# Linear attention followed by attention experts on one core: batch 0's k loads from ScalarE's queue, the table load behind them, fewer zero matmuls in front

## The chip, the core and the metric

The kernel runs on one core of one Trainium2 chip. TensorE (PE) multiplies matrices, VectorE (DVE), ScalarE (ACT) and GpSimd (POOL) work elementwise, and SyncE (SP) mostly starts transfers (DMA). Any of SyncE, ScalarE and GpSimd can start a transfer. Each engine works through its own list of instructions in order and waits on semaphores for the others. The metric is the device time of one execution in microseconds (us); the figure given is the median of the runs.

## The reference

```python
kv  = einsum('bhsd,bhse->bhde', k, v)          # batch 8, heads 8, seq 576, head_dim 64
o   = einsum('bhsd,bhde->bhse', q, kv)
x   = o / sqrt(mean(o*o) + 1e-6) * g_norm      # per head; heads side by side: (8, 576, 512)
logits = x @ w_gate                            # 4 experts, the best 2 of each token
for e in range(4):                             # causal attention of each expert
    a   = softmax(mask(scale * (x @ wq[e]) @ (x @ wk[e]).T))
    out += weight_of(e) * (a @ (x @ wv[e]) @ wo[e])
```

All inputs and the output are float32.

## The kernel before

The eight batches are worked one after the other, with neighbouring batches overlapping. The body of the kernel is a list of some 1,100 small tasks, each a name and indices, such as ("kv", 0, 2). The list's order is written out by hand in `ORDER`, and `ENGINE` says for every task which engine runs it (V, A, G, S, and C for ScalarE's own queue). The loop at the end (L840 to L844) walks through it and emits each task. So each engine's instructions stand in the order of the list, and an engine never passes one of its own instructions over to a later one.

Transfers in the front are cut small. k and v of one batch come as four loads each, `lk(b, p, z)` and `lv(b, p, z)`: p picks the heads (0 to 3 or 4 to 7), z the first 4 or the last 5 of the 9 neighbouring rows that go to one partition (256 KB for z = 0, 320 KB for z = 1). q comes as two loads `lq(b, u)` of 576 KB. `load` at L328 issues those of k and v on SyncE (L332), `lq` those of q (L347). Partitions of z = 0 have a fifth column that no load fills; it is set to zero by a memset (L218, L219, L223, L224), and the loads with z = 1 write into the same column and so wait for that memset.

The order in which batch 0 begins, with each task's engine, is this:

- SyncE: lv(0,1,0), lv(0,1,1), lk(0,1,1), lk(0,1,0), lq(0,1): the "first half", heads 4 to 7
- TensorE: kv(0,2), kv(0,3) (`kv`, L408): the products of k and v of heads 4 to 7, which need all four loads of p = 1
- ScalarE: kvc(0,1) (L419, the copy to `kvs` by `copy`, L311)
- SyncE: lv(0,0,0)
- ScalarE: kvx(0,3,1) (L424, a copy of 32 partitions to `kvm`)
- VectorE: kvx(0,1,1)
- SyncE: lk(0,0,1), lv(0,0,1)
- VectorE: kvx(0,2,1)
- SyncE: lk(0,0,0)
- ScalarE: kvx(0,0,1)
- TensorE: o(0,1) (`o_mm`, L442), which needs all of `kvs`, `kvm` and the transposed q (VectorE, L437)
- ScalarE: the squares of o (L470)
- TensorE: kv(0,0), kv(0,1), which need the "second half" of k and v, heads 0 to 3; then the sums of the squares (L482), from which the norm is worked out in turns of ScalarE and VectorE
- SyncE: lq(0,0), and then the loads of batch 1: lk(1,1,1), lv(1,0,1), lv(1,0,0), lk(1,0,0), lk(1,1,0), lv(1,1,0), lk(1,0,1), lv(1,1,1), the k weights, q of batch 1

Before some tasks stand zero matmuls (`zero_matmuls`, L826): products of a tile of zeros, written to a bank that the task behind them overwrites. `ZEROS` (L26) says before which task and how many. [...] ScalarE's table of functions is loaded by the instruction at L217, ahead of everything else on ScalarE.

Eight semaphores serve the transfers of SyncE and ScalarE in turn, in the order of the list. A transfer whose semaphore still belongs to an earlier one waits until that one has landed.

Of the kernel before, what the change touches and what calls it, by code (L numbers as in the profile page):

```python
# [23 lines left out]


ZEROS = {  # L26
    ("kv", 0, 2): 20, ("o", 0, 1): 6, ("kv", 0, 0): 2, ("o", 0, 0): 2,
}

ORDER = (  # L30
# [96 lines left out]
def kernel(  # L127
# [13 lines left out]
    nc = tc.nc  # L141
# [22 lines left out]
    order_only = mybir.DependencyInfo(mybir.DependencyClass.Sync, mybir.DependencyReason.DATA)  # L164
    begun = [0]
    moved = []

    def place(key, n=1):
        if key not in slot_of:
            at = begun[0]  # L170
            slot_of[key] = tuple(int(d, 16) for d in SLOTS[at : at + n])
            begun[0] += n
        return slot_of[key]
# [40 lines left out]
    kt, vt = [  # L214
        [sb.tile([P, H, LO + 1, Dh], FP32, tag=f"{m}{j}", name=f"{m}_b{j}") for j in range(2)] for m in "kv"
    ]
    nc.scalar.preload_act_table_set("natural_log_exp_and_others")  # L217
    nc.gpsimd.memset(vt[0][:, :, LO], 0.0)  # L218
    nc.vector.memset(kt[0][:, :, LO], 0.0)  # L219
    ident_f = const.tile([P, P], FP32, name="ident_f")  # L220
# [56 lines left out]
    for j in range(2):  # L277
        t = const.tile([P, NCH * S + PAD], FP32R, name=f"xT{j}")
        nc.vector.tensor_copy(out=t[:, NCH * S :], in_=zeros[:, 0:PAD])
        xTs.append(t)  # L280
    for j in range(3):
        t = const.tile([P, 2, strips + PAD], BF16, name=f"PT{j}")
        nc.gpsimd.memset(t[:, :, strips:], 0.0)
        PTs.append(t)
        t = const.tile([P, NB * P], FP32R, name=f"kT{j}")
        nc.vector.tensor_copy(out=t[:, S:], in_=zeros[:, 0:PAD])
        kTs.append(t)
    for j in range(2):
        t = const.tile([P, NB, 8], FP32, name=f"lg8_{j}")
        nc.gpsimd.memset(t[:], -1.0e30)  # L290
        lg8s.append(t)
        t = const.tile([P, NB, E, Hd + 1], BF16, name=f"vext{j}")
# [30 lines left out]
    def queued(task, ins):  # L323
        if len(task) > 1 and task[0] in ("lk", "lv", "lq") and task[1] > 1:
            tc.add_manual_dep(ins.ins, moved[-FLIGHT].name, order_only, reason="queue")
        moved.append(ins.ins)

    def load(m, dst, src, b, p, z):  # L328
        n, t0 = LO + z, LO * z
        hs = slice(4 * p, 4 * p + 4)  # L330
        rows = src[b, hs].rearrange("h (r t) d -> r h (t d)", t=RUN)[:, :, t0 * Dh : (t0 + n) * Dh]
        queued((m, b), nc.sync.dma_start(dst[z::2, hs, 0:n, :].rearrange("r h t d -> r h (t d)"), rows))  # L332

    def lk(b, p, z):
        load("lk", k_t(b), k, b, p, z)

    def lv(b, p, z):
        load("lv", v_t(b), v, b, p, z)
# [469 lines left out]
    def store(b, qc, *h):  # L808
# [8 lines left out]
        lk=lk, lv=lv, lq=lq, lgv=lgv, lwg=lwg, wgs=wgs, lw=lw, ws=ws, lwo=lwo, wo=wo, kv=kv, kvc=kv_copy, kvx=kv_move, qc=q_turn,  # L817
        o=o_mm, oc=o_copy, sq=square, ms=sums, G=gates, ln=ln, rs=rs, na=newton_a, nb=newton_b, lo=newton_c, R=newton_d,
# [7 lines left out]
    def zero_matmuls(n, count):  # L826
        if n[0] in ("kv", "v", "y", "ot", "lt", "ms", "G"):
            at = (kv_bank(*n[1:]) if n[0] == "kv" else small("v", n[1], n[2] // 2) if n[0] == "v" else small(*n))[0]
        elif n[0] in ("qp", "kp"):
            at = small(n[0][0], *n[1:])[0]  # L830
        elif n[0] == "o":
            at = big("o", n[1], n[2], 0)[0]
        else:
            at = big(*n)[0]
        for _ in range(count):
            use(nc.tensor.matmul(  # L836
                bank(at)[:, 2 * P : 3 * P], lhsT=zeros[:, 0:P], rhs=zeros[:], start=True, stop=True, skip_group_check=True
            ), at)

    with tc.manual_schedule():  # L840
        for n in order:
            if n in ZEROS:
                zero_matmuls(n, ZEROS[n])
            emit[n[0]](*n[1:])  # L844
# [30 lines left out]
```

## Time and profile before

| | |
|---|---|
| median of 3 runs | 202.35 us (202.04 to 202.89) |
| the profiled execution: its own time | 203.93 us |
| the profiled execution: its span, first to last instruction | 202.2 us |
| mean granted TensorE clock | 0.984 |
| batch 0's k loads, issued by SyncE at | 2.31, 2.96, 4.92, 6.80 us |

Times in the profile count from the start of the span. In a row of a timeline the first number is the start and the second the length in us, then come the engine, the line of the kernel, the operation and what it writes from what; "x2" says that two instructions in a row are merged, and the bracket gives the idle time before it and what ended it. "SPq" is SyncE issuing transfers, "PEld" TensorE's loading of weights. In a row of stretches each engine has its busy time and, in brackets, the number of instructions; behind them stand the granted TensorE clock as a share of full speed, the share of time that the 16 DMA engines were busy, and GB/s. In a list of transfers the last number is the time from issue to landing. In a list of who waited for whom, the numbers are the total, how often, and the longest wait.

### The profile page before, as it was taken

The numbers are of one execution on the slowest core, as the hardware profiler recorded it, in microseconds if no ns is written. First come the engines' busy times: TensorE is split into PE (matmuls) and PEld (weight loads), VectorE is DVE, ScalarE is ACT, GpSimd is POOL, SyncE is SP. The second block draws the span as 40 slices with busy tenths as digits, with TensorE's granted clock in tenths as the row PEclk, the third lists the DMA queues.
The fourth block names the chain that finished last, engine by engine and source line by source line (L and its number), as shares of the span: only waits on it lengthen the run. The fifth ranks groups of instructions, "written<-read, shape, count | busy, mean of one in ns | idle before, by whom it ended". The sixth has DMA issues, their size and how long they took to land.

```text
span 202.2 us, 7076 instructions
## 1 busy us (share of the span) xinstructions
PE 188.7 (93%) x2917; PEld 153.2 (76%) x2934; DVE 135.5 (67%) x336; ACT 129.6 (64%) x240; POOL 70.3 (35%) x185
## 2 busy tenths in 40 slices
PE   7599889999999999999999999999999999999980
PEld 7486475789689698679878797879867878988740
DVE  7035899977566866857695558666877696667640
ACT  2016627577768588953966969796477657567960
POOL 8201163203373441408253541165026224126500
PEclk9969999999999999999999999999999999999996
DMA  4999987998899699850189930100044134025595
GB/s 151 293 366 350 329 194 177 326 389 257 275 375 339 157 379 363 268 173 3 17 252 383 348 115 3 55 3 0 3 156 159 63 109 143 3 95 179 198 348 175
DMA packets 33808, 40.31 MB, mean 199 GB/s; under 512 B 8288, under 2 KB 24944, under 8 KB 33776
## 3 DMA queue, kind: packets, MB, share of 16 engines
q1 hardware_dynamic: 33248, 39.20, 59.1%
q10 hardware_dynamic: 432, 0.66, 0.9%
q8 instruction: 23, 0.38, 0.8%
q14 instruction: 9, 0.07, 0.1%
q0 software_dynamic: 96, 0.01, 0.1%
HBM read 30.42 MB, written 9.44 MB: 197 GB/s over the span
## 4 chain that ended last, share of the span: by engine, by line
PE 74%; DVE 8%; ACT 5%; DMA 5%; issue 4%; POOL 1%; SPq 0%; DVEq 0%; ACTq 0%; POOLq 0%
PE banks L643 13%; PE banks L414 9%; PE banks L674 8%; PE banks L450 8%; PE banks L482 8%; PE banks L624 7%; PE banks L719 6%; PE banks L794 6%; DMA k_b<-in_k_dram 3%; PE banks L563 3%; DVE qT L437 3%; PE banks L762 2%; PE banks L836 2%; DMA out_dram<-stage 2%; PE banks L545 1%
## 5 line engine op out<-in xcount | busy, mean ns | idle before, releaser
L686 ACT ACTIVATE PT<-banks 128x1024 bf16<-128x1024 f32 (+1 forms) x64 | 51.7, 836 | 11.2 <-PE banks L674 9.7
L693 POOL TENSOR_SCALAR_AFFINE_SELECT PT<-PT 128x256 bf16<-128x256 bf16 (+1 forms) x80 | 28.9, 382 | 20.7 <-ACT PT L686 20.4
L437 DVE STREAM_TRANSPOSE qT<-q_b 128x576 f32<-128x576 f32 x32 | 23.6, 756 | 8.2 <-DMA q_b<-in_q_dram 5.9
L571 DVE TENSOR_TENSOR xT<-banks,ob 128x576 fp32r<-128x576 f32 x32 | 23.4, 746 | 4.6 <-PE banks L563 4.4
L624 PE MATMUL banks<-wv_r,xT 128*128 128x256 f32 x160 | 24.5, 290 | 0.0
L414 PE MATMUL banks<-v_b,k_b 128*64 128x64 f32 x640 | 21.1, 224 | 2.5 <-DMA k_b<-in_k_dram 2.5
L414 PEld LDWEIGHTS banks<-v_b,k_b 128*64 128x64 f32 x640 | 19.7, 138 | 4.6 <-issue 3.0
L643 PE MATMUL banks<-xT,wk_r 128*128 128x288 f32 x128 | 22.3, 307 | 0.1
L624 PEld LDWEIGHTS banks<-wv_r,xT 128*128 128x128 f32 x160 | 21.2, 189 | 1.4 <-DVE wv_r L387 0.2
L643 PE MATMUL banks<-xT,wq_r 128*128 128x288 f32 x128 | 22.1, 305 | 0.1
L674 PE MATMUL banks<-qTp,kT 64*128 64x192 f32 (+3 forms) x224 | 21.3, 307 | 0.0
L674 PEld LDWEIGHTS banks<-qTp,kT 64*128 64x128 f32 x224 | 15.8, 185 | 5.5 <-issue 2.0
L643 PEld LDWEIGHTS banks<-xT,wk_r 128*128 128x128 f32 x128 | 18.4, 188 | 1.8 <-ACT ob L311 0.5
L643 PEld LDWEIGHTS banks<-xT,wq_r 128*128 128x128 f32 x128 | 18.2, 188 | 1.9 <-DVE kT L312 0.5
L450 PE MATMUL banks<-qT,kvs 32*64 32x288 f32 x256 | 19.1, 412 | 0.4 <-DVE g_den L608 0.3
L474 POOL TENSOR_TENSOR sqs<-ob 128x576 f32<-128x576 f32 x14 | 16.1, 1155 | 7.7 <-DVE ob L312 4.9
L719 PEld LDWEIGHTS <-PT 128*128 128x128 bf16 x480 | 15.8, 97 | 3.4 <-DVE ob L312 0.9
L450 PE MATMUL banks<-qT,kvm 32*64 32x288 f32 x256 | 18.3, 411 | 0.0
L794 PE MATMUL banks<-wo_b,OT 128*128 128x512 bf16 (+1 forms) x57 | 16.6, 372 | 1.6 <-issue 1.0
L311 ACT COPY stage<-banks 128x512 f32<-128x512 f32 x25 | 14.1, 593 | 5.4 <-PE banks L794 4.1
L719 PE MATMUL banks<-vext,PT 128*128 128x65 bf16 x480 | 17.4, 193 | 0.0
L311 ACT COPY ob<-banks 128x576 f32<-128x576 f32 x19 | 11.8, 637 | 8.3 <-PE banks L450 8.3
(95 smaller groups left out, 301.1 us busy)
## 6 DMA issues: line engine op xcount, KB each, us to landing
q_b<-in_q_dram SPq DMA_DIRECT2D x16, 576.0 KB, 6.9
out_dram<-stage SPq DMA_DIRECT2D x29, 256.0 KB, 2.5
v_b<-in_v_dram SPq DMA_DIRECT2D x16, 320.0 KB, 6.4
k_b<-in_k_dram SPq DMA_DIRECT2D x16, 320.0 KB, 5.5
v_b<-in_v_dram SPq DMA_DIRECT2D x16, 256.0 KB, 6.2
k_b<-in_k_dram SPq DMA_DIRECT2D x16, 256.0 KB, 5.9
out_dram<-stage SPq DMA_DIRECT2D x9, 128.0 KB, 2.7
stage<-in_moe_wk_dram SPq DMA_DIRECT2D x2, 256.0 KB, 7.1
```

What stands on the lines that cost most here:

```text
L311: return nc.scalar.copy(dst, src)
L414: use(nc.tensor.matmul(p_kv[hh * Dh : (hh + 1) * Dh, c, :], lhsT=k_t(b)[:, h, j, :], rhs=v_t(b)[:, h, j, :], start=(j == 0), stop=(j == LO ...
L437: nc.vector.transpose(q_part(b, dh)[:, ms].rearrange("p m (t i) -> p m t i", t=RUN), q_t(b)[:, ms, :, dh * 32 : (dh + 1) * 32],)
L450: use(nc.tensor.matmul(bank(n)[at : at + Dh, 0:HALF], lhsT=(kvs if z == dh else kvm)[b % 2][pp, m], rhs=q_part(b, dh)[pp, m], start=(dh == ...
L571: use(nc.vector.tensor_tensor(out=xTs[b % 2][:, 0 : NCH * S].rearrange("p (n s) -> p n s", s=S)[:, cs, cols], in0=both(ns)[:, :, 0:HALF], ...
L624: use(nc.tensor.matmul(bank(n)[:, at : at + E * Hd], lhsT=blocks_of(xTs[b % 2], c)[:, i * P : (i + 1) * P], rhs=w_r["v"][:, c, :, :].rearr ...
L643: use(nc.tensor.matmul(bank(n)[:, 0:HALF], lhsT=w_r[nm][:, c, 2 * pr : 2 * pr + 2, :].rearrange("p e f -> p (e f)"), rhs=blocks_of(xTs[b % ...
L674: use(nc.tensor.matmul(bank(ns[el])[:, o : o + hi - lo], lhsT=kTs[(2 * b + pr) % 3][pp, kb * P : (kb + 1) * P], rhs=tiles["qTp", b, pr][pp ...
L686: use(nc.scalar.activation(PTs[(2 * b + pr) % 3][:, :, 512 * j : 512 * j + o], both(ns)[:, :, 0:o], ACTF.Exp, scale=scale), *ns)
L693: nc.gpsimd.affine_select(out=d, in_=d, compare_op=AluOpType.is_ge, fill=0.0, base=0, pattern=[[0, 2], [1, w]], channel_multiplier=-1,)
L719: use(nc.tensor.matmul(heads[el][:, k_ * W1 : (k_ + 1) * W1], lhsT=PT[:, el, col : col + P], rhs=vexts[b % 2][:, kb, 2 * pr + el, :], star ...
L794: use(nc.tensor.matmul(bank(n)[:, 0 : cols.stop - cols.start], lhsT=OT[:, pr, at : at + P], rhs=wo_b[:, pr, cols], start=(pr == 0), stop=( ...
```

## The change

Three edits. First, the four loads of batch 0's k are issued on ScalarE's queue; all other loads stay on SyncE. The order of the list is the same. Second, ScalarE's table load is emitted just ahead of kvc(0,1) instead of ahead of everything. Third, 23 zero matmuls stand in front instead of 30: 15 for 20 before kv(0,2), 5 for 6 before o(0,1), 1 for 2 before kv(0,0), and 2 as before ahead of o(0,0).

```diff
 ZEROS = {
-    ("kv", 0, 2): 20, ("o", 0, 1): 6, ("kv", 0, 0): 2, ("o", 0, 0): 2,
+    ("kv", 0, 2): 15, ("o", 0, 1): 5, ("kv", 0, 0): 1, ("o", 0, 0): 2,
 }
...
+    preloaded = []
...
-    nc.scalar.preload_act_table_set("natural_log_exp_and_others")
...
-        queued((m, b), nc.sync.dma_start(dst[z::2, hs, 0:n, :].rearrange("r h t d -> r h (t d)"), rows))
+        q_ = nc.scalar if (m, b) == ("lk", 0) else nc.sync
+        queued((m, b), q_.dma_start(dst[z::2, hs, 0:n, :].rearrange("r h t d -> r h (t d)"), rows))
...
         for n in order:
+            if n[0] == "kvc" and n[1] == 0 and not preloaded:
+                preloaded.append(1)
+                nc.scalar.preload_act_table_set("natural_log_exp_and_others")
             if n in ZEROS:
                 zero_matmuls(n, ZEROS[n])
             emit[n[0]](*n[1:])
```

## The prediction

> **What bounds the kernel now.** I read the page first, then the chain of waits of the first 32 us, because all edits lie in front, then who waited for whom, and then single transfers and the granted clock of that stage. The page:
>
> ```profile
> span 202.2 us, 7076 instructions
> ...
> PE 188.7 (93%) x2917; PEld 153.2 (76%) x2934; DVE 135.5 (67%) x336; ACT 129.6 (64%) x240; POOL 70.3 (35%) x185
> ...
> PE 74%; DVE 8%; ACT 5%; DMA 5%; issue 4%; POOL 1%; SPq 0%; DVEq 0%; ACTq 0%; POOLq 0%
> ```
>
> TensorE is busy in 93% of the span and carries 74% of the chain that ended last. A delay of its front is therefore a delay of the end, unless a later wait for something with a time of its own swallows it. The chain of waits in the front (start, length, what):
>
> ```profile
> 2.31 0.61 SPq L332
> ...
> 2.96 6.80 DMA k_b<-in_k_dram
> 9.76 0.14 issue
> 9.90 1.40 PE banks L414 x40
> ...
> 11.32 0.27 ACT kvs L311
> ...
> 11.64 2.93 PE banks L836 x12
> 14.57 1.21 PE banks L450 x32
> ...
> 16.41 1.31 PE banks L414 x40
> 17.73 1.12 PE banks L482 x8
> ```
>
> Read downwards: SyncE issues the first half of k, lk(0,1,0), at 2.96; it lands at 9.76; TensorE multiplies kv(0,2) and kv(0,3) from 9.90; ScalarE copies out (kvc(0,1)) at 11.32; 12 zero instructions fill until 14.57; o(0,1) runs; 4 zero instructions; kv(0,0) and kv(0,1) from 16.41 to 17.72, and from there products, ScalarE and VectorE steps in turn. The second half of k is not on this chain. Who waited for whom in the whole run:
>
> ```profile
> PE banks L414 <- DMA k_b<-in_k_dram: 2.5, 1, 2.5
> ```
>
> TensorE waited visibly for a transfer once, 2.5 us, for this k. No later transfer is waited for by it, so no later slack would take up a shift of the front; I count it one to one to the end.
>
> **The change, part by part.** The sum goes from event to event on the span's clock up to the end of kv(0,1), 17.72 before. SyncE's issues now:
>
> ```profile
> 0.80 1.46 SPq L332 DMA_DIRECT2D v_b<-in_v_dram  x2
> 2.31 1.27 SPq L332 DMA_DIRECT2D k_b<-in_k_dram  x2
> 3.62 0.61 SPq L347 DMA_DIRECT2D q_b<-in_q_dram  x1
> ...
> 4.92 0.62 SPq L332 DMA_DIRECT2D k_b<-in_k_dram  x1
> ...
> 6.80 1.29 SPq L332 DMA_DIRECT2D k_b<-in_k_dram  x1
> ...
> 9.82 2.12 SPq L332 DMA_DIRECT2D v_b<-in_v_dram  x2
> 12.26 1.61 SPq L332 DMA_DIRECT2D k_b<-in_k_dram  x2
> ...
> 14.91 0.60 SPq L332 DMA_DIRECT2D k_b<-in_k_dram  x1
> ```
>
> **Where the four loads stand.** One issue takes 0.61 to 0.65. The first half of k is issued at 2.31 and 2.96, the second at 4.92 and 6.80. In the written order, however, lk(0,0,1) and lk(0,0,0) come behind kvc(0,1) and kvx(0,3,1), and these two are ScalarE's. On SyncE that did not matter; SyncE passed neither. On ScalarE, which works in order, they cannot be issued before kvc(0,1) has its result:
>
> ```profile
> 0.80 1.28 ACT L217 ACT_TABLE_LOAD   x1 [0.80 <-PEq L859]
> 11.32 0.27 ACT L311 COPY kvs<-banks 128x128 f32<-128x128 f32 x1 [9.24 <-PE banks L414]
> 11.62 0.61 ACT L311 COPY kvm<-kvs 32x128 f32<-32x128 f32 x2
> ```
>
> So the second half moves from 4.92 and 6.80 to behind the copy that begins at 11.32 now. This is the main term.
>
> **The table load** (1.28) goes behind the first half's two issues, about 3.0 to 4.3. ScalarE's next work is kvc(0,1) at 11.32: price 0, covered by the wait for k; without that cover 1.28.
>
> **The first half's landing (A).** Its first issue waits for the memset of k's fifth column:
>
> ```profile
> 1.12 0.48 DVE L219 MEMSET k_b<- 128x512 f32 x1
> ```
>
> That ends at 1.60, so ScalarE can issue at 1.65 and 2.30 instead of 2.31 and 2.96: 0.66 earlier. The landings, each row one transfer, from issue to landing (issued at 1.63, 2.31, 3.62, 2.96, 6.80):
>
> ```profile
> v_b<-in_v_dram SPq DMA_DIRECT2D x1, 320.0 KB, 3.4
> ...
> k_b<-in_k_dram SPq DMA_DIRECT2D x1, 320.0 KB, 5.1
> ...
> q_b<-in_q_dram SPq DMA_DIRECT2D x1, 576.0 KB, 7.7
> ...
> k_b<-in_k_dram SPq DMA_DIRECT2D x1, 256.0 KB, 6.8
> ...
> k_b<-in_k_dram SPq DMA_DIRECT2D x1, 256.0 KB, 8.1
> ```
>
> Lower bound: lk(0,1,0) lands with the 5.1 of the k load ahead of it: 2.30 + 5.1 = 7.40, A = -2.36. With its own 6.8: 9.10, A = -0.66. Against it: SyncE, freed of two issues, issues q's first half (576 KB) at 2.31 instead of 3.62, beside lk(0,1,0) instead of behind it. Both queues feed the same DMA engines, and these are already at a share of 0.90 and 0.95 (rows below). If all of q goes ahead, k lands when q lands now, 3.62 + 7.7 = 11.32: A = +1.56. I take the middle of -0.66 and +1.56, A = +0.45: about half of q's bytes get in between. The first half lands at 10.21.
>
> The Trainium skill (DMA: Bandwidth & Descriptors, section "Issuing engines are not separate DMA queues") says that transfers started by different engines run interleaved on the same 16 DMA engines, and that starting them from several saves only the time of issue. By that rule A could not be better than -0.66, and with -0.66 the sum would be 1.11 less, 203.4; that the DMA engines are already this busy agrees with it.
>
> **Zero matmuls and the clock (B).** Each is two instructions. The rows of the granted clock, cut at 3.41 us from the clock's own changes (stretch, length, busy time of each engine, clock, DMA), and the first block:
>
> ```profile
> 1.02:4.44 3.42, 3.32 (x15) 3.32 (x16) 3.19 (x24) 1.06 (x1) 3.33 (x15) 1.00 0.55 172
> 4.44:7.85 3.41, 2.98 (x27) 2.79 (x25) 0.97 (x4) 0.00 (x0) 1.68 (x3) 1.00 0.90 293
> 7.85:11.26 3.41, 1.36 (x40) 1.28 (x40) 0.00 (x0) 0.00 (x0) 0.00 (x0) 1.00 0.95 303
> 11.26:14.68 3.42, 3.06 (x21) 2.82 (x28) 1.88 (x4) 0.86 (x3) 0.00 (x0) 0.50 1.06 376
> 14.68:18.09 3.41, 3.41 (x80) 2.45 (x81) 1.49 (x3) 1.48 (x4) 0.00 (x0) 1.00 1.09 357
> 18.09:21.50 3.41, 2.53 (x43) 1.23 (x38) 2.35 (x6) 2.81 (x7) 0.57 (x2) 1.00 1.10 317
> ```
>
> ```profile
> 1.12 6.30 PE L836 MATMUL banks<-zeros 128*128 128x128 f32 x40 [1.12 <-DVE zeros L210]
> ```
>
> Fifteen zero instructions run up to 4.44 (0.22 each), the other 25 in 2.98 (0.119 each), ending at 7.42. With 15 zero matmuls, 30 instructions, the block ends at 4.44 + 15 x 0.119 = 6.23. The five that are left out lie in TensorE's wait for k: price 0 by themselves. But the stretch 7.85 to 11.26, busy for 1.36, is followed by clock 0.50; those busy for 2.53 and more are followed by 1.00. After the change the stretch 4.44 to 7.85 is busy for 1.79, nearer to 1.36. So I expect the clock to fall at 7.85, and kv(0,2) and kv(0,3) to run at half rate: the zeros take 0.244 at 0.50 (12 in 2.93) against 0.119. Bounds 0 and twice the length, +1.40; by the nearer row B = +1.40. The fall at 11.26 is paid before as well.
>
> The Trainium skill (TensorE: Matmul & The Clock Gate, Part 1) puts the fall after at least one idle window of about 3.4 us. Taken as a wholly idle window there would be none here, B = 0, the rival "clock holds" with 203.1; the trace speaks against that form, since the stretch with 1.36 of work was followed by the fall.
>
> kvc(0,1) starts at 11.32 + 0.45 + 1.40 = 13.17.
>
> **The second half's landing (C).** ScalarE then dispatches kvc(0,1) and kvx(0,3,1) and issues lk(0,0,1): between 0 and 0.6 after (the copy and the first of the two kvm copies end at about 11.93); I take 0.30, 13.47. lk(0,0,0) follows 0.65 later, 14.12. Its time to land: at least 3.4 (a load with one other in flight), at most the 8.1 that it takes now. Before, SyncE keeps the DMA engines fed: at 9.82 its issue follows the landing at 9.76 at once, and the next, inside the same 2.12, that of q at 11.32: a load waits for the one eight places before it. After, lk(1,1,0) is eight places behind lk(0,0,1) and SyncE stops there, so little stands before k. I take 4.25, the middle of the 3.4 and the 5.1 of loads with little ahead. It lands at 18.37.
>
> **TensorE's side.** Ten zeros instead of 12 start at 13.49: five at 0.244 to 14.68, five at 0.119 to 15.3; o(0,1) 1.2; two zeros: TensorE is ready for kv(0,0) at 16.8, and waits 1.6. The zeros left out in front of o and kv(0,0) (2 x 0.244 and 2 x 0.119) thus give nothing. kvx(0,0,1) stands behind the two issues, done at about 13.17 + 0.30 + 1.30 + 0.31 = 15.1, under the zeros: 0; without them it would be up to 0.4. The squares behind it come after o(0,1).
>
> kv(0,0) starts 0.14 after the landing, as it did at 9.90, at 18.51, and ends 1.40 later at 19.91, against 17.72: **+2.2**.
>
> **SyncE's stop** delays batch 1's loads: lk(1,1,0), the second of the two in the row of 12.26 (about 13.3), goes when lk(0,0,1) lands, about 17.7: 4.4 later, and with it those behind. Who needs them:
>
> ```profile
> 24.34 3.10 POOL L387 TENSOR_SCALAR wk_r<-stage,g_part 128x256 fp32r<-128x256 f32 x3 [5.54 <-DMA stage<-in_moe_wk_dram]
> ```
>
> ```profile
> 24.45 1.39 PE L414 MATMUL banks<-v_b,k_b 128*64 128x64 f32 x40
> ...
> 28.88 1.29 PE L643 MATMUL banks<-xT,wk_r 128*128 128x288 f32 x8
> ```
>
> The last k load of batch 1 is issued at 14.91 now; with the 8.1 above it lands at 23.0 and is used at 24.45, which itself moves by 2.2: cover 3.6 against 4.4, less what an emptier queue saves on the way (8.1 to 4.25). GpSimd scales the k weights as they land, to 27.44, for the projection at 28.88: cover 1.4 + 2.2 by the same count. Bounds 0 and 1; I take 0, by the emptier queue.
>
> The profiled execution took 203.93 with a span of 202.2, so 1.73 lie around the span, and the change touches none of it: 206.1 for a profiled one. The median shown is 202.35; plus 2.2 is **204.5**.
>
> **The rivals.** (1) **k early, the other side: faster.** ScalarE's own queue is served beside v instead of behind it, the first half lands at 7.40, no idle stretch long enough for a fall at 7.85: kvc(0,1) at 7.40 + 0.14 + 1.40 + 0.02 = 8.96, issues at 9.26 and 9.91, landing 14.16, kv(0,1) done at 15.70: -2.0, **200.3**. It decides as soon as the first half lands before about 9.4 at full clock; for 0.5%, before 8.4. For it: 5.1 occurs in the same stage. Against it: DMA share 0.90, and q pulled forward.
> (2) **Gain in front, loss behind: no change.** Only the 0.66 of issue, clock held: kvc(0,1) at 10.66, landing 15.86, done at 17.40: -0.3, **202.0**.
> (3) **Clock holds**, else as forecast: kvc(0,1) at 11.77, landing 16.97, done at 18.51: +0.8, **203.1**. For it: 1.79 is more than 1.36.
> (4) **The second half queues as now**, 8.1: landing 22.22, done at 23.76: +6.0, **208.4**; a second fall of the clock during that wait would do part of the same. Against it: SyncE's stop.
> That the change doesn't do what it says: the front loads do leave from ScalarE; what fails is only that two of the four leave later than before.
>
> **How the numbers follow.** Forecast 0.42, rival 1 0.16, rival 2 0.12, rival 3 0.18, rival 4 0.12. About 0.5%, 1.0 us, can be told from no change here (runs shown 202.04 to 202.89). Faster: rival 1 and 0.02 of rival 2, 0.18. Same: the rest of rival 2 and 0.11 of rival 3, 0.21. Slower: 0.61. The outer bounds of all terms together would be about 199 to 210; 201.2 to 207.0 leaves out some 0.10 of rival 1 and 0.09 of rival 4. The forecast's own range, A from -0.66 to +1.56, is 203.4 to 205.6.
>
> **What would show it.** Right: ScalarE's DMA issues three and four directly behind the kvs copy and one kvm copy; TensorE waiting for k a second time, before kv(0,0); SyncE standing at a batch-1 k load until then; clock 0.50 from about 7.85. The whole forecast is wrong if lk(0,0,0) lands before TensorE has finished o(0,1); A is wrong if the first half lands before 9.1, B if kv(0,2) runs its 40 instructions in 1.4.

## The result and the profile after

| | before | after |
|---|---|---|
| median | 202.02 us (201.69 to 202.89, 6 runs) | 209.31 us (208.78 to 211.54, 6 runs) |
| ratio | | 1.0378 (95% interval 1.0323 to 1.0433) |
| span of the profiled execution | 202.2 us | 209.2 us |
| mean granted TensorE clock | 0.984 | 0.970 |

The change makes the kernel 3.8% slower: 7.3 us between the two medians, 7.6 us by the ratio. The page of the changed kernel (its code stands one line lower from the edit on, so L414 is now L415, L643 is L644):

```profile
span 209.2 us, 7065 instructions
...
PE 191.0 (91%) x2920; PEld 153.1 (73%) x2920; DVE 135.7 (65%) x336; ACT 129.7 (62%) x240; POOL 69.9 (33%) x185
...
PE 74%; DMA 9%; DVE 8%; ACT 3%; issue 2%; ACTq 1%; POOL 0%; DVEq 0%; POOLq 0%
```

Of the 7.0 by which the span is longer, TensorE stands still for 4.7 (18.2 in all against 13.5). The other 2.3 is longer busy time (191.0 against 188.7) at a lower mean clock (0.970 against 0.984). On the chain, transfers hold 9% where they held 5%. The chain of waits of the first 30 us (start, length, what):

```profile
1.69 0.66 ACTq L333
...
2.38 9.31 DMA k_b<-in_k_dram
11.69 0.14 issue
11.83 2.42 PE banks L415 x40
...
14.26 0.28 ACT kvs L311
...
14.85 0.32 ACTq L333
...
15.22 7.05 DMA k_b<-in_k_dram
...
22.31 2.16 PE banks L415 x40
24.47 1.92 PE banks L483 x8
...
26.41 0.50 ACT root L502
```

Two transfers of k stand on it now instead of one: 9.31 from 2.38, and 7.05 from 15.22. Event by event:

| event | before | after | later by |
|---|---|---|---|
| first half of k landed | 9.76 | 11.69 | 1.93 |
| kvc(0,1) starts | 11.32 | 14.26 | 2.94 |
| kv(0,0) starts | 16.41 | 22.31 | 5.90 |
| sums of squares (L482, L483) start | 17.73 | 24.47 | 6.74 |
| logarithm on ScalarE (L501, L502) starts | 18.87 | 26.41 | 7.54 |
| projection kp (L643, L644) starts | 28.88 | 36.41 | 7.53 |

The whole loss is there when the logarithm starts, and up to the projection the kernel runs as before, shifted. Who waited for whom, and the projection:

```profile
PE banks L415 <- DMA k_b<-in_k_dram: 9.2, 2, 5.0
```

```profile
36.41 1.29 PE L644 MATMUL banks<-xT,wk_r 128*128 128x288 f32 x8
```

TensorE's waits for k are two and 9.2 in sum, where there was one of 2.5. SyncE's and ScalarE's lists in the front:

```profile
2.30 0.61 SPq L348 DMA_DIRECT2D q_b<-in_q_dram  x1
...
6.16 1.28 SPq L333 DMA_DIRECT2D k_b<-in_k_dram  x1
11.75 1.26 SPq L333 DMA_DIRECT2D v_b<-in_v_dram  x2
13.07 1.26 SPq L333 DMA_DIRECT2D k_b<-in_k_dram  x2
21.74 0.60 SPq L333 DMA_DIRECT2D v_b<-in_v_dram  x1
```

```profile
1.64 1.56 ACTq L333 DMA_DIRECT2D k_b<-in_k_dram  x2
3.23 1.28 ACT L845 ACT_TABLE_LOAD   x1 [3.23 <-issue]
...
14.56 0.29 ACT L311 COPY kvm<-kvs 32x128 f32<-32x128 f32 x1
14.57 1.28 ACTq L333 DMA_DIRECT2D k_b<-in_k_dram  x2
15.89 0.30 ACT L311 COPY kvm<-kvs 32x128 f32<-32x128 f32 x1 [1.04 <-issue]
```

ScalarE issues its third and fourth load at 14.57 and 15.22, right behind the dispatch of kvc(0,1) and of one kvm copy, and the other kvm copy waits behind the two issues until 15.89, 1.04 idle. SyncE does nothing from 7.44 to 11.75, then issues four loads of batch 1 (lv, lv, lk, lk) until 14.3, and then stands until 21.74. The granted clock, in stretches cut where this execution's clock changes:

```profile
5.58:8.99 3.41, 1.27 (x11) 1.07 (x10) 0.00 (x0) 0.00 (x0) 0.36 (x1) 1.00 0.93 298
8.99:12.40 3.41, 0.57 (x11) 0.60 (x13) 1.38 (x3) 0.00 (x0) 0.00 (x0) 0.50 0.97 328
...
15.82:19.23 3.41, 2.29 (x40) 1.42 (x39) 0.76 (x1) 1.49 (x3) 0.00 (x0) 1.00 0.86 277
19.23:22.64 3.41, 0.33 (x10) 0.34 (x12) 2.08 (x3) 0.00 (x0) 0.00 (x0) 1.00 0.08 24
22.64:26.06 3.42, 3.42 (x45) 2.20 (x40) 0.00 (x0) 0.86 (x3) 0.57 (x2) 0.50 0.77 238
```

The clock fell twice in the front: at 8.99, after a stretch with 1.27 of work, and at 22.64, after one with 0.33, the wait for the second half.

### The profile page after: what moved, and what is told of

Its sections match the earlier page's. It is cut to its first block, busy times and chain, and to the rows that moved or that the text cites. A ratio compares the mean times of both kernels' runs of the same rounds, so it can differ in the third digit from the quotient of the medians.

```text
span 209.2 us, 7065 instructions
## 1 busy us (share of the span) xinstructions
PE 191.0 (91%) x2920; PEld 153.1 (73%) x2920; DVE 135.7 (65%) x336; ACT 129.7 (62%) x240; POOL 69.9 (33%) x185
## 3 DMA queue, kind: packets, MB, share of 16 engines
HBM read 30.42 MB, written 9.44 MB: 191 GB/s over the span
## 4 chain that ended last, share of the span: by engine, by line
PE 74%; DMA 9%; DVE 8%; ACT 3%; issue 2%; ACTq 1%; POOL 0%; DVEq 0%; POOLq 0%
PE banks L644 14%; PE banks L415 9%; PE banks L675 9%; PE banks L483 8%; PE banks L625 8%; DMA k_b<-in_k_dram 8%; PE banks L451 7%; PE banks L720 7%; PE banks L795 6%; PE banks L564 2%; DVE qT L438 2%; PE banks L763 2%; DMA out_dram<-stage 2%; PE banks L546 1%; ACT stage L311 1%
## 5 line engine op out<-in xcount | busy, mean ns | idle before, releaser
L415 PE MATMUL banks<-v_b,k_b 128*64 128x64 f32 x640 | 22.6, 234 | 9.2 <-DMA k_b<-in_k_dram 9.2
L415 PEld LDWEIGHTS banks<-v_b,k_b 128*64 128x64 f32 x640 | 21.2, 147 | 11.2 <-issue 5.3
L644 PE MATMUL banks<-xT,wk_r 128*128 128x288 f32 x128 | 22.3, 307 | 0.1
L644 PE MATMUL banks<-xT,wq_r 128*128 128x288 f32 x128 | 22.0, 305 | 0.1
L795 PE MATMUL banks<-wo_b,OT 128*128 128x512 bf16 (+1 forms) x74 | 20.2, 375 | 0.0
L644 PEld LDWEIGHTS banks<-xT,wk_r 128*128 128x128 f32 x128 | 18.4, 188 | 1.8 <-ACT ob L311 0.5
L644 PEld LDWEIGHTS banks<-xT,wq_r 128*128 128x128 f32 x128 | 18.2, 188 | 1.9 <-DVE kT L312 0.5
L451 PE MATMUL banks<-qT,kvm 32*64 32x288 f32 x256 | 18.2, 410 | 0.0
```

The lines of the kernel that those rows point to most:

```text
L415: use(nc.tensor.matmul(p_kv[hh * Dh : (hh + 1) * Dh, c, :], lhsT=k_t(b)[:, h, j, :], rhs=v_t(b)[:, h, j, :], start=(j == 0), stop=(j == LO ...
L451: use(nc.tensor.matmul(bank(n)[at : at + Dh, 0:HALF], lhsT=(kvs if z == dh else kvm)[b % 2][pp, m], rhs=q_part(b, dh)[pp, m], start=(dh == ...
L644: use(nc.tensor.matmul(bank(n)[:, 0:HALF], lhsT=w_r[nm][:, c, 2 * pr : 2 * pr + 2, :].rearrange("p e f -> p (e f)"), rhs=blocks_of(xTs[b % ...
L795: use(nc.tensor.matmul(bank(n)[:, 0 : cols.stop - cols.start], lhsT=OT[:, pr, at : at + P], rhs=wo_b[:, pr, cols], start=(pr == 0), stop=( ...
```

## The experiments

Theories: the **order theory** (the loss is the second half of k, which ScalarE can issue only behind kvc(0,1)), the **sharing theory** (k on a second queue runs against SyncE's loads) and the **zeros theory** (fewer zero matmuls let the clock fall). The ratios are to the kernel before, run on the same chip, and the us behind a ratio are that share of its median there. By the same count the whole change costs 7.6 us.

**Only the first half on ScalarE**, everything else as changed:

```diff
-        q_ = nc.scalar if (m, b) == ("lk", 0) else nc.sync
+        q_ = nc.scalar if (m, b, p) == ("lk", 0, 1) else nc.sync
```

> The changed kernel, but only the first half of batch 0's k (lk(0,1,1), lk(0,1,0)) is issued by ScalarE; the second half goes back to SyncE. Order theory (the loss comes from the second half standing behind kvc(0,1) on ScalarE): no second wait of TensorE for k, no second fall of the clock; what stays is the later first half and the slower kv in front, kv(0,1) done at about 19 instead of 24.5, 203 to 204 us. Sharing theory (any k on ScalarE's queue runs against SyncE's loads, and that is the loss): nearly as slow as the change, 207 or more. Zeros theory (fewer zero matmuls let the clock fall, and that is the loss): 207 or more too.

Ratio 1.0109 (1.0066 to 1.0152), some 2.2 us, a little more than expected (203 to 204 is at most 1.7 over the 202.35 of before). Its chain of waits:

```profile
2.38 8.86 DMA k_b<-in_k_dram
...
18.14 1.31 PE banks L415 x40
19.45 1.12 PE banks L483 x8
```

The second wait for k is gone, kv(0,0) starts at 18.14 instead of 22.31. The first half still lands late, at 11.24 (2.38 + 8.86). So the second half's place makes more than two thirds of the loss (5.4 of 7.6), and the rest stays with the first half, the zeros and the table load.

**Only the second half on ScalarE**, in the kernel before:

```diff
-        queued((m, b), nc.sync.dma_start(...))
+        q_ = nc.scalar if (m, b, p) == ("lk", 0, 0) else nc.sync
+        queued((m, b), q_.dma_start(...))
```

> The kernel before, but only the second half of batch 0's k (lk(0,0,1), lk(0,0,0)) is issued by ScalarE; zeros and table load as before. Order theory: kvc(0,1) at 11.3 as before, the second half issued at 11.6 and 12.3, landed some 7 later at about 19.3, kv(0,1) done at 20.7 to 21.5, 205 to 206.5 us. Zeros theory: 202. Sharing theory: 202 to 203, since the first half is alone on SyncE's queue.

Ratio 1.0315 (1.0257 to 1.0373), 6.4 us: the order theory, and more than it gave. Its chain of waits:

```profile
10.50 0.28 ACT kvs L311
...
11.55 8.25 DMA k_b<-in_k_dram
...
19.84 2.40 PE banks L415 x40
22.24 1.42 PE banks L483 x8
```

Here the first half came early (kvc(0,1) at 10.50), and the second half's last load still landed at 19.80, 8.25 after its issue. TensorE then ran kv(0,0) and kv(0,1) in 2.40 instead of 1.31, at a fallen clock. The two parts' 2.2 and 6.4 add up to more than the whole 7.6. In the profiled executions they do not: there the logarithm starts 1.72 late with the first half alone (20.59) and 4.81 with the second half alone (23.68), 6.53 together, against 7.54 with both. The profiled execution of the second half alone was the fastest of its four. So the parts do not add up exactly, and why is open.

**All four issued early by ScalarE**: the second half moved in the list to right behind the first, otherwise the change.

```diff
+    for n in (("lk", 0, 0, 0), ("lk", 0, 0, 1)):
+        order.remove(n)
+        order.insert(order.index(("lk", 0, 1, 0)) + 1, n)
```

> The changed kernel with the second half of k moved in the written order to right behind the first half, so that ScalarE issues all four loads at 1.6 to 4.3, ahead of the table load and kvc(0,1). Order theory: the second half has landed long before kv(0,0); only the later first half and the clock in front stay, 203 to 204.5 us. Sharing theory: 207 or more. Zeros theory: 207 or more.

Ratio 1.0135 (1.0087 to 1.0182), 2.7 us: with all four loads on ScalarE's queue but ahead of kvc(0,1), 4.9 of the 7.6 are back. In its chain of waits kv(0,0) and kv(0,1) follow behind o(0,1) without a wait for k:

```profile
17.44 1.32 PE banks L418 x40
```

For these 4.9 it is the place in the list that costs, not the queue. The 2.7 that are left, somewhat more than expected (203 to 204.5 us), are about what the first half alone costs.

**30 zero matmuls** with the change's other edits:

```diff
-    ("kv", 0, 2): 15, ("o", 0, 1): 5, ("kv", 0, 0): 1, ("o", 0, 0): 2,
+    ("kv", 0, 2): 20, ("o", 0, 1): 6, ("kv", 0, 0): 2, ("o", 0, 0): 2,
```

> The changed kernel with the 30 zero matmuls of before. Zeros theory: back to 202 to 204 us. Order theory: the wait for the second half stays and the clock falls in it again; at best kv(0,2) runs at full clock, 1.0 less, 208 to 209.5 us.

Ratio 1.0297 (1.0243 to 1.0351), 6.0 us: the wait stays. The intervals of this run and of the whole change overlap, so whether the zeros are worth any of the 1.6 between them is not shown. Its granted clock, in stretches cut at its own changes:

```profile
7.27:10.68 3.41, 1.50 (x13) 1.31 (x12) 1.00 (x2) 0.00 (x0) 0.00 (x0) 1.00 0.88 286
10.68:14.10 3.42, 2.11 (x46) 2.00 (x47) 2.35 (x13) 0.56 (x2) 0.00 (x0) 1.00 0.97 345
...
17.50:20.93 3.43, 0.41 (x14) 0.41 (x16) 2.24 (x4) 0.00 (x0) 0.00 (x0) 1.00 0.44 153
20.93:24.34 3.41, 3.41 (x42) 2.05 (x38) 0.00 (x0) 0.86 (x3) 0.57 (x2) 0.50 0.93 252
```

With 20 zero matmuls ahead of it, kv(0,2) ran at full clock in this execution: the stretch with 1.50 of work was not followed by a fall. The one with 0.41, in the wait for the second half, was.

**The change without its queue edit**: all loads on SyncE, 23 zeros, the later table load.

```diff
-        q_ = nc.scalar if (m, b) == ("lk", 0) else nc.sync
+        q_ = nc.sync
```

> The change without its edit of the queue: all loads of batch 0's k on SyncE, but 23 zero matmuls and the later table load. Order theory: nothing of the loss is left, kvc(0,1) at 11.3 or up to 1.0 later where the clock falls early, 202 to 203.5 us. Zeros theory: a good part of the 7 stays, 204 or more.

Ratio 0.9972 (0.9928 to 1.0017): no difference that shows. The zeros theory falls as the cause of the loss; without the queue edit no cost of the other two shows. In its profiled execution kv(0,2) and kv(0,3) ran at full clock, with 15 zero matmuls ahead of them:

```profile
9.57 1.39 PE L415 MATMUL banks<-v_b,k_b 128*64 128x64 f32 x40 [3.05 <-DMA k_b<-in_k_dram]
```

**SyncE's q held back**: the first half alone on ScalarE, and lq(0,1) waits until lv(0,1,1) has landed. SyncE works in order, so its later loads wait with it.

```diff
+        if len(moved) == 4:
+            tc.add_manual_dep(ins.ins, moved[1].name, order_only, reason="queue")
```

> The first half alone on ScalarE (second half on SyncE), and SyncE's lq(0,1) held until lv(0,1,1) has landed, about 5, so that q does not run beside the first half of k. If q between k's pieces is what made the first half land at 11.3 to 11.7 instead of 9.8: it lands at 8 to 9.8, kv(0,1) done 1.5 to 3 earlier than with the first half alone, 201 to 203 us. If ScalarE's queue is slow in itself: 11 or later, 205 us.

Ratio 0.998 (0.9943 to 1.0017); no loss shows any more, where the first half alone cost 2.2. The time to landing of lk(0,1,0), issued at 2.38 as with the change:

```profile
k_b<-in_k_dram ACTq DMA_DIRECT2D x1, 256.0 KB, 5.5
```

5.5 instead of 9.3, landed at 7.89. ScalarE's queue is not slow in itself; with SyncE's next loads kept out of the way until 5.13, k comes earlier than in any of the executions here that load it from SyncE (8.20 at best). So the 2.2 of the first half alone come from SyncE's loads beside k. That gains nothing, because now q is late. Its chain of waits:

```profile
5.13 5.68 DMA q_b<-in_q_dram
...
10.84 1.45 DVE qT L440 x2
...
12.33 2.47 PE banks L453 x32
```

**Batch 1's loads held back** in the changed kernel until ScalarE's copy behind its two issues:

```diff
+    by_task, held = {}, []
...
+        if task == ("lk", 1) and not held:
+            held.append(task)
+            tc.add_manual_dep(ins.ins, by_task["kvx", 0, 0, 1].name, order_only, reason="queue")
...
-            copy(task, dst, src)
+            by_task[task] = copy(task, dst, src).ins
```

> The changed kernel with SyncE's loads of batch 1 held until ScalarE has issued the second half of k (until its copy kvx(0,0,1) behind the two issues). If the five loads of batch 1 in front of it made the second half take 7.05: issued at about 15.2 as in the change, landed in 3.4 to 4.5, at about 19.5, kv(0,1) done at 20.8 to 21.8, 3 less than the change at this place; later waits for batch 1's loads may give part of that back, 205 to 208 us. If ScalarE's queue is slow in itself, or one DMA engine behind: 6.5 or more to landing, 209 us or more.

Ratio 1.0213 (1.0151 to 1.0275), 4.3 us instead of 7.6. The time to landing of lk(0,0,0), issued at 14.98, and the chain of waits behind it:

```profile
k_b<-in_k_dram ACTq DMA_DIRECT2D x1, 256.0 KB, 4.4
```

```profile
19.73 1.62 PE banks L419 x40
21.35 1.12 PE banks L487 x8
```

With batch 1's loads out of the way the load takes 4.4 instead of 7.05. So holding them back took 2.6 off its time. kv(0,0) then starts at 19.73, and no longer because of k, which landed at 19.41: TensorE came to it only then, since the clock had fallen at 10.13, stayed at 0.50 until 20.37, and o(0,1) took 2.15 where it took 1.21 before.

**The small loads on SyncE**, in the kernel before: one of the sixteen parts of the first half lands far behind the rest.

```diff
-            nc.gpsimd.dma_start(g_part[h * Dh : (h + 1) * Dh], g_norm.unsqueeze(1))
+            nc.sync.dma_start(g_part[h * Dh : (h + 1) * Dh], g_norm.unsqueeze(1))
...
-        nc.gpsimd.dma_start(wg_in[:], moe_w_gate.rearrange("(n p) e -> p n e", p=P))
+        nc.sync.dma_start(wg_in[:], moe_w_gate.rearrange("(n p) e -> p n e", p=P))
```

> The kernel before, with the three small loads of g and w_gate issued by SyncE at their places in the list instead of by GpSimd. In the profile before, one of the sixteen parts of lk(0,1,0) lands at 9.76, fourteen by 7.4. If GpSimd's small loads hold up that DMA engine: the first half lands at about 7.5 to 8.5, 200 to 201.5 us. If not: 9 to 10 as before, 202 us.

Ratio 0.9939 (0.9907 to 0.9971): 1.2 us faster than before, the fastest version here. lk(0,1,0), issued at 2.97:

```profile
k_b<-in_k_dram SPq DMA_DIRECT2D x1, 256.0 KB, 5.2
```

5.2 to landing, at 8.20, against 6.8 before. One execution is not enough to say that the small loads held k up: with the two versions of it below that leave the first half on SyncE, it landed at 8.52 and 9.01. The gain is measured, its cause is open.

**That version with the k weights earlier** (their first load ahead of lv(1,1,0) and lv(1,1,1)):

```diff
+    for n in (("lv", 1, 1, 1), ("lv", 1, 1, 0)):
+        order.remove(n)
+        order.insert(order.index(("lw", "k", 0)) + 1, n)
```

> The kernel before with the small loads of g and w_gate on SyncE, and the first load of the k weights moved ahead of lv(1,1,0) and lv(1,1,1). With the small loads alone on SyncE, kp waited for GpSimd's scaling of those weights, which landed at 23.4. If that is what bounds the front now: they land some 1.5 earlier, kp starts up to 0.8 earlier, 200 to 201 us against 202.5 of before. If the order of batch 1's v matters more: 201.5 or later.

Ratio 0.9951 (0.992 to 0.9981): 1.0 us faster than before, less than the 1.5 to 2.5 of the first expectation, and not told apart from the small loads alone. The weights landed at 22.16 instead of 23.42, but kp started no earlier (27.22, against 26.87 for the bulk of it with the small loads alone): they do not bound the front by themselves.

**That version with 23 zero matmuls**:

```diff
-    ("kv", 0, 2): 20, ("o", 0, 1): 6, ("kv", 0, 0): 2, ("o", 0, 0): 2,
+    ("kv", 0, 2): 15, ("o", 0, 1): 5, ("kv", 0, 0): 1, ("o", 0, 0): 2,
```

> The kernel before with the small loads of g and w_gate on SyncE and the 23 zero matmuls of the change. Zeros theory: where k comes early, fewer zeros in front of o(0,1) and kv(0,0) gain up to 0.5 against the small loads alone, 200.5 to 201.3 us. Order theory: the zeros are worth nothing either way, the same as with the small loads alone, about 201.3.

Ratio 0.9967 (0.9933 to 1.0001): no gain from fewer zeros.

**That version with the first half on ScalarE and q held** (and the change's zeros and table load):

```diff
+        if len(moved) == 4:
+            tc.add_manual_dep(ins.ins, moved[1].name, order_only, reason="queue")
...
+        q_ = nc.scalar if (m, b, p) == ("lk", 0, 1) else nc.sync
```

> The first half of k on ScalarE with SyncE's lq(0,1) held until lv(0,1,1) has landed, and the small loads of g and w_gate on SyncE. Both causes of a late first half are gone: it lands at 7.0 to 7.9. If o(0,1) then waits for q instead, which lands at 10 to 10.8: no better than the small loads alone, 201 to 202 us. If k still set the pace: 200 to 201 us.

Ratio 0.9977 (0.9942 to 1.0012). The first half landed at 7.41, and o(0,1) waited for q, which landed at 10.59. k and q both have to be there for o(0,1); bringing k forward at the cost of q moves the wait.

## Why the prediction had the right direction and a time far too small

**Direction and place: right.** The loss was put down to the second half standing behind kvc(0,1), with two ScalarE issues directly behind the dispatch of the copies, a second wait of TensorE, and SyncE standing. All of it is in the profile after, though SyncE stood at lv(1,1,0) and not at a load of k; the third and fourth issue lie 0.31 and 0.96 behind the start of kvc(0,1), 0.30 and 0.95 were forecast. The runs with one half at a time show it.

**The time: too small, +2.2 for +7.3.** The sum ended with kv(0,1) done at 19.91; it was done at 24.47. The 4.56 between them, by term:

| term | forecast | measured | difference |
|---|---|---|---|
| A, first half's landing, later by | 0.45 | 1.93 | +1.48 |
| B, clock in kv(0,2), kv(0,3) | 1.40 | 1.02 (2.42 against 1.40) | -0.38 |
| C, time to landing of lk(0,0,0) | 4.25 | 7.05 | +2.80 |
| kv(0,0) and kv(0,1) themselves, from landing | 1.54 | 2.20 | +0.66 |

**C is the step that failed**: the time to landing of lk(0,0,0), put at 4.25, was 7.05. The prediction said that SyncE would stop at lk(1,1,0), eight places behind lk(0,0,1), "so little stands before k". That does not follow even by its own count. Ahead of lk(1,1,0) stand lv(1,0,1), lv(1,0,0) and lk(1,0,0), and the first of them is eight places behind lk(0,1,0), forecast to land at 10.21. So these three loads could leave only from 10.21 on, directly ahead of ScalarE's issue at 13.47. In the profile SyncE did stand for the landing of the first half, and four loads of batch 1 came in one burst at 11.75 to 14.3, directly ahead of ScalarE's issues at 14.57. The fourth is lk(1,1,0): in the trace it has the semaphore of lv(0,0,1), landed at 13.05, and lv(1,1,0) has that of lk(0,0,1). So the semaphores do not go in the order of the list there.

Holding batch 1's loads back gives 4.4, close to the 4.25. Part of the 7.05 is one DMA engine. The trace has sixteen landings for each load; fifteen of those of lk(0,0,0) had come by 20.59, 5.37 behind the issue, and the last came at 22.26. With batch 1's loads held back these were 3.38 behind the issue and 1.05 more. With 30 zeros the load took 6.46 behind the same burst, with the last part only 0.08 behind the fifteenth. So the burst is enough to make k late, and what the one engine adds differs from execution to execution.

The rival in which the second half queues as it did on SyncE (8.1, 208.4 us) was the right case and got 0.12. That its time comes near is in part luck: 8.1 is 1.05 too long, while A is 1.48 too short in it as well and the second fall of the clock is left out of its sum.

**A was mis-sized**, beyond its upper bound of +1.56. The cause was named in part: q goes beside k instead of behind it. In the profile after, q's half and lk(0,1,0), from issue to landing:

```profile
q_b<-in_q_dram SPq DMA_DIRECT2D x1, 576.0 KB, 8.7
k_b<-in_k_dram ACTq DMA_DIRECT2D x1, 256.0 KB, 9.3
```

q (issued at 2.30) landed first, k 0.7 behind it. The forecast took half of q's bytes in between, the bound all of them. But SyncE's loads behind q went beside k as well: of lv(0,0,0), issued at 2.95, fifteen of sixteen parts had landed by 11.05. From 4 to 11 us SyncE's queue moved 1.44 MB, of which q's half makes at most 0.59, and ScalarE's queue the 0.59 of k. Holding q and all that is behind it brings k at 7.89, which shows that SyncE's loads are the cause; q was not held alone, so its own share is not shown. The Trainium skill (DMA: Bandwidth & Descriptors, section "Issuing engines are not separate DMA queues") says that transfers of several engines interleave on the same DMA engines and that only the time of issue is saved. The runs agree: 0.58 of issue were gained (2.38 for 2.96), and the landing, beside SyncE's loads, took 9.31 instead of 6.80, so that it came 1.93 later.

**B came about, but not by the stretch it was argued from.** The clock's stretches begin at another place in each execution: they are cut at 4.44 before and at 5.58 after. After, a stretch with 1.27 of work was followed by the fall. The 1.79 of the argument was read as near enough to 1.36; with 30 zeros a stretch with 1.50 was not followed by one. But busy time alone does not decide it in these traces: with q held back the clock fell behind a stretch with 1.88, and in the version with the small loads on SyncE and 23 zeros behind one with 2.09. In the execution without the queue edit, also with 15 zeros there, kv(0,2) and kv(0,3) took 1.39 and the clock did not fall. B was worth 1.02 here and 0 there, and with one execution of each the number of zeros is not told apart from where the stretches happen to begin.

**The second fall** of the clock was named only as part of a rival. It cost 0.85 in kv(0,0) and kv(0,1) (2.16 against 1.31) and 0.80 in the sums of squares (1.92 against 1.12), the latter behind the point at which the sum ended: 24.47 + 1.94 gives the logarithm's 26.41, 7.54 late.

**Priced at nothing, rightly:** the table load (3.23 to 4.51, ScalarE idle behind it until 14.26), the kvm copy behind the two issues, the zeros left out (TensorE waits anyway), and batch 1's late loads: kp is 7.53 late, just as the logarithm is, so they added nothing. Of the 7.54, the span shows 7.0; where the 0.5 came back is open.

## What to carry to other kernels

Before an instruction is moved to another engine's list, read what stands ahead of it there: a load that is issued far ahead of its use on SyncE can end up behind a copy that itself waits for the load's own neighbour. The second queue of the change brought no load sooner, with the DMA engines already at a share of 0.90 and more: what is issued in the freed places goes beside the load that was to hurry, so the first queue has to be held back too, and then its loads are the late ones. A wait in front of TensorE costs more than its length when the clock falls behind it, here 1.65 more.

## What was unexpected of the hardware

**One DMA engine behind.** In the wait for the second half, these stretches (length, busy times, clock, DMA share, GB/s) and, from 17.5 to 22, two of the DMA queues (packets, MB, share of 16 engines):

```profile
18.00:19.00 1.00, 0.12 (x2) 0.00 (x0) 0.53 (x1) 0.98 (x2) 0.00 (x0) 1.00 0.78 277
19.00:20.00 1.00, 0.00 (x0) 0.00 (x0) 0.97 (x3) 0.00 (x0) 0.00 (x0) 1.00 0.24 72
20.00:21.00 1.00, 0.00 (x0) 0.00 (x0) 1.00 (x3) 0.00 (x0) 0.00 (x0) 1.00 0.08 28
21.00:22.00 1.00, 0.00 (x0) 0.00 (x0) 0.34 (x1) 0.00 (x0) 0.00 (x0) 1.00 0.06 19
```

```profile
q10 hardware_dynamic: 455, 0.48, 30.7%
...
q8 instruction: 1, 0.02, 2.1%
```

From 20 to 22 the share is 0.08 and 0.06, about one engine of sixteen, at 28 and 19 GB/s: from 20.59 on fifteen had finished, and TensorE waited for one until 22.26. In the same stretch one engine had fetched a 16 KB piece of instructions, 2.1% of 16 engines in 4.5 us, which is 1.5 us. The fetch began at 17.7; the last part of lk(1,0,0), landed at 18.36, came 0.71 behind the fifteenth, that of lk(1,1,0) right after it 2.48. That the fetch put the engine behind is a guess: in the kernel before, one of the same size at 15.1 left the last parts as late as they had been (1.35 to 1.43).

**One part late, whoever issues the small loads.** With the three small loads on GpSimd lk(0,1,0) landed at 9.76, 9.44 and 8.94 in the executions that left the first half on SyncE; with them on SyncE at 8.20, 8.52 and 9.01. The two sets touch. How far the last of the sixteen parts came behind the fifteenth does differ, 1.69, 1.56 and 1.15 against 0.85, 0.36 and 0.64. But with the first half on ScalarE and the small loads on GpSimd it was anything from 0.14 to 1.64 in six executions. So GpSimd's loads are at most a part of what holds one engine up; the rest is open.
